# A recurrent gated attention with a feed-forward block on one core: a planned order of steps replaced by another

## The chip, the cores and the metric

The kernel runs on one core of one Trainium2 chip. The time is device microseconds of one execution of the whole program. The core has five engines with an instruction queue each: TensorE (PE), VectorE (DVE), ScalarE (ACT), GpSimd (POOL) and SyncE (SP), which only issues transfers here. Each engine runs its own queue in order, and waits for the others by semaphores.

## The reference

```python
def _attn_ref(q, k, v, alpha):              # (4, 8, 768, 48) each
    B, H, S, D = q.shape
    state = np.zeros((B, H, D, D), dtype=np.float32)
    y = np.zeros_like(q)
    for t in range(S):
        state = alpha[:, :, t, :, None] * state + np.einsum('bhd,bhe->bhde', k[:, :, t], v[:, :, t])
        y[:, :, t] = np.einsum('bhd,bhde->bhe', q[:, :, t], state)
    return y.astype(np.float32)

def _moe_ref(x, w_in, w_out):               # (3072, 384), (384, 2048), (2048, 384)
    h = x @ w_in
    g = h * np.cos(h)
    return (g @ w_out).astype(np.float32)
```

The output of the recurrence, with heads side by side, is the `x` of the second function. The result is 3072 x 384 in float32.

## The kernel before

*Tiling.* The sequence of 768 steps of each of 4 batches is cut into three pieces of 256, so there are 12 such pieces over all; the code calls the index `J`, and this text calls each a pair, because it holds two chunks (`c` = 0 and 1) of 128 steps. Within a chunk, steps lie two to a partition: the even or odd step is `e`. All 8 heads of 48 are handled together.

*The recurrence of a pair, step by step.* `load` brings alpha, k, q, v (393 KB each) through SP's queue. `mula` (line 149, POOL) multiplies neighbouring alphas, from pair 3 on. `ln` (L141, ACT) takes logarithms; `cums0` and `cums` (L155, L167, PE) sum them with triangular matrices; `sub` (L182, DVE) makes the sums of even steps from those of odd ones; `icp` and `exps` (L192, L200, ACT) take exponentials of both signs, and `eb` is these four and the next pair's `ln` as one step. `sk` and `sq` (L212, L216) scale k and q by them, on DVE where the plan has `:D`, else on POOL. `castv` (L219, POOL) makes v bfloat16; its two halves are stacked into `vs` by four transfers of SP (`vst`, L225) or, for pairs 0 to 2, by products with the identity (`vpe`, L235, and an eviction `vev`, L239). `decay` (L244, POOL) prepares the chunk's decay. `trans` (L260, PE) transposes k and q, `evT` (L266) evicts its two halves, `scores` (L274, PE) and `mask` (L279, DVE) make the masked scores of each chunk, `outer` (L291, PE) the outer products of k and v, `add` (L305, L307, DVE) and `state` (L313, POOL) the running state, `yT` (L340, PE) the output of the recurrence, transposed, and `evy` (L350) evicts its halves into `xT`.

*The feed-forward block of a pair.* `m1` (L359, PE) makes four units `h_ps` of 128 x 1024 (12 products each); `sin` (L365, ACT) their cosine; `gate` (L370, DVE) the product of the two; `m2` (L387, PE; L381 for the last chunk) multiplies by the second weight in four parts per chunk; `evo` (L396) evicts a chunk's result, and `out` (L403) stores it. The weights come through POOL's queue, in four quarters each (`w1`, `w2`; L121, L127), as needed first by pair 0.

*Buffers.* Most products write one of three PSUM buffers (tag `h`, two banks each: `h_ps`, `T_ps`, `A_ps`, `U_ps`, `y_ps`, `vs_ps`, and the first sums). A product that takes such a buffer waits until what was in it has been read: `m1` waits for a `gate` or a `mask` three uses earlier, for example. `m2` has one buffer (tag `o`), `cums` from pair 3 on one (tag `x`). The second half of a tile that is written by another engine waits for the first half (`evT 0` and `evT 1` write one tile, `evy 0` and `evy 1` too).

*Products of zeros.* `idle` (L411) multiplies zeros by zeros into a buffer that nothing reads, as often as the plan says, during the first 19 us.

*What sets the order.* A table, `PLAN` (L428 to L493), has a row for each kind of step (with the chunk, half or unit as second word) and a number for each of the 12 pairs; a letter behind a number names the engine (`A` ACT, `D` DVE; POOL or the step's own engine without one). The steps are issued in the order of these numbers over all rows, with the products of zeros (`IDLE`: number, how many) among them. So the numbers only sort: every engine's queue, SP's and POOL's too, is the part of this one list that it has to run. They are no times of the chip. The load of pair 2's alpha is also made to wait for the last product of `yT` of pair 1 (`GATES`, L99).

Of the kernel before, what the change touches and what calls it, by code (L numbers as in the profile page):

```python
# [16 lines left out]
def kernel(  # L17
# [11 lines left out]
    B, H, S, D = q.shape  # L29
# [64 lines left out]
    w1 = consts.tile([C, KT, DF], BF, tag="w1", name="w1")  # L94
    w2 = consts.tile([C, NF, DM], BF, tag="w2", name="w2")
# [311 lines left out]
    def idle(n):  # L407
# [21 lines left out]
        "load a": "1320 1974 27415 27985 34270 40270 43270 54870 67336 68770 70970 93397",  # L429
        "load k": "750 2544 28555 37270 46270 52480 58570 69470 72470 85140 91627 113474",  # L430
        "load q": "5250 6750 29125 38770 48970 56370 57870 60070 78470 84570 87104 96187",
        "load v": "3750 8250 35770 41770 51910 61570 67906 73970 75470 85710 95267 96757",
        "w1": "15334 12769 17804 16954",
        "w2": "11919 20284 19434 21134",
        "mula": "- - - 36680 41180 47582 54280 61956 76220 87867 79850 105765",
        "ln": "6160 7660 35857 38802 - - - - - - - -",
        "cums0": "7065 8565 36762 - - - - - - - - -",
        "cums": "7385 8885 37082 40224 45645 52564 65189 75864 86319 101370 105687 126624",
        "sub": "- - - 41095 48653 53084 68143 79971 86910 101948 106207 127144",
        "icp 0": "8400 10365 37282 - - - - - - - - -",  # L440
        "icp 1": "9990 9615 38042 - - - - - - - - -",
        "exps 0": "11510 9085 37657 - - - - - - - - -",
        "exps 1": "10740 11125 38417 - - - - - - - - -",
        "eb": "- - - 43138 49360 59320 71283 83790 88947 103219 109067 127741",
        "sk 0": "8970:D 11125:D 38180 44230 53330 64626 74150 90547 93387 106715 109595 129364:D",
        "sk 1": "10655:D 10185:D 38612:D 45094:D 52380 60226 77170 88817 96837 110545 113395 132041",
        "sq 0": "12160:D 14753:D 40150:D 45680:D 56671:D 65155:D 78900 85074 95107 111495 112445 133161",
        "sq 1": "12974:D 14283:D 39680:D 45680 55230 63676 75100 86024 91497 114515 116415 129403",
        "castv": "10660 16184 42680 48680 62906 71716 73380 94337 92617 104995 130491 144063",
# [90 lines left out]
```

## Time and profile before

| | |
|---|---|
| three runs | 189.58, 189.61, 190.51 us (median 189.61) |
| the profiled execution, its own time | 189.73 us |
| its span, first to last instruction | 187.7 us |
| granted TensorE clock, mean | 0.997 |
| TensorE busy from 0 to 22.2, 22.2 to 122, 122 to 187.7 us | 18.78, 96.96, 61.45 us |
| DVE, ACT, POOL busy over the span | 134.3, 125.3, 77.4 us |
| share of the 16 DMA engines, 0 to 100 us | 1.0 or more in each stage (0.69 from 100 to 122, 0.20 behind) |
| transfers | 29.47 MB in 60537 packets, 51424 of them under 512 B |

The profile is one execution. Its page has the busy time of each engine, the work in 40 slices, the transfer queues, the chain of work that ended last, and the costliest groups of instructions; the trace behind it gives each instruction's start and length and who ended a wait. A line of a timeline reads: start in us, length in us, engine, source line, operation, output and inputs, how many were merged, and in brackets the idle time before it and what ended that. Lengths of products are modelled at their end, so that neighbouring ones overlap. A row of waits reads: who waited for whom, us in total, how often, the longest.

### The profile page before, as it was taken

The page shows a single profiled execution, that of the slowest core. Times are in us where ns is not written, and L with a number is a line of the kernel's source. Part 1 is how long each engine was busy: PE and PEld are TensorE (multiplying, and loading weights), DVE is VectorE, ACT ScalarE, POOL GpSimd, SP SyncE. Part 2 cuts the span into 40 slices and gives each one's busy share as a digit, 9 for nine tenths or more (in the row PEclk, how much of TensorE's full clock was granted, in tenths as well). Part 3 has the DMA queues.
Part 4 walks back from the last instruction along what each step waited for, and adds up shares of the span by engine and source line. Part 5 has one row for each costly group of instructions (what it writes and reads, how often), then busy time and mean ns, then how long its engine had stood idle before and what let it go on. Part 6 is the DMA issues. An engine that isn't in the chain of part 4 may idle for free.

```text
span 187.7 us, 5795 instructions
## 1 busy us (share of the span) xinstructions
PE 177.2 (94%) x2471; PEld 126.7 (67%) x2474; DVE 134.3 (72%) x184; ACT 125.3 (67%) x161; POOL 77.4 (41%) x110
## 2 busy tenths in 40 slices
PE   7997799998999999999999999999999999999990
PEld 2444678664577776775688668686776786776880
DVE  7069775589799899589657986885876666573550
ACT  2466876899598977788577999728956182372520
POOL 5059610257664733783894068830540310100000
PEclk9999999999999999999999999999999999999998
DMA  6999999999959988996799943600042005501303
GB/s 152 261 256 154 185 203 236 255 264 265 249 137 302 265 184 217 265 268 166 195 280 259 216 106 90 166 0 3 3 114 73 0 21 124 128 1 45 84 0 84
DMA packets 60537, 29.47 MB, mean 157 GB/s; under 512 B 51424, under 2 KB 60512, under 8 KB 60512
## 3 DMA queue, kind: packets, MB, share of 16 engines
q1 hardware_dynamic: 56640, 25.86, 59.8%
q0 software_dynamic: 3712, 3.15, 11.0%
q8 instruction: 19, 0.31, 0.7%
q10 hardware_dynamic: 160, 0.10, 0.2%
q14 instruction: 6, 0.05, 0.1%
HBM read 25.17 MB, written 4.72 MB: 159 GB/s over the span
## 4 chain that ended last, share of the span: by engine, by line
PE 71%; ACT 16%; DVE 7%; issue 3%; DVEq 0%
PE h_ps L359 31%; PE o_ps L387 23%; PE idle_ps L411 5%; PE y_ps L340 3%; ACT c_sb L365 3%; ACT qkT L266 3%; DVE gsb L370 3%; PE T_ps L260 2%; ACT cp L200 2%; ACT L136 2%; ACT L365 2%; PE A_ps L274 2%; PE U_ps L291 2%; ACT lna L141 2%; ACT icp L192 2%
## 5 line engine op out<-in xcount | busy, mean ns | idle before, releaser
L370 DVE TENSOR_TENSOR gsb<-h_ps,c_sb 128x1024 bf16<-128x1024 f32 x48 | 58.1, 1221 | 22.3 <-ACT c_sb L365 21.5
L365 ACT ACTIVATE c_sb<-h_ps,halfpi 128x1024 bf16<-128x1024 f32 x48 | 53.0, 1113 | 27.4 <-PE h_ps L359 23.4
L359 PE MATMUL h_ps<-xT,w 128*128 128x256 bf16 x576 | 66.7, 273 | 1.4 <-issue 0.6
L387 PE MATMUL o_ps<-w,gsb 128*128 128x384 bf16 x368 | 66.7, 326 | 0.0
L359 PEld LDWEIGHTS <-w 128*128 128x128 bf16 x576 | 55.6, 98 | 10.4 <-issue 1.9
L387 PEld LDWEIGHTS <-gsb 128*128 128x128 bf16 x368 | 33.8, 98 | 21.2 <-DVE gsb L370 0.6
L313 POOL TENSOR_TENSOR un<-us,c 128x384 bf16<-128x384 f32 x20 | 16.8, 843 | 40.3 <-DVE us L305 33.9
L279 DVE TENSOR_TENSOR A_sb<-A_ps,msk 128x1024 bf16<-128x1024 f32 x24 | 28.9, 1216 | 1.3 <-PE A_ps L274 1.3
L212 POOL TENSOR_TENSOR kh<-k,icp 128x384 bf16<-128x384 f32 x17 | 16.9, 999 | 8.7 <-ACT icp L192 8.7
L216 POOL TENSOR_TENSOR qh<-q,cp 128x384 bf16<-128x384 f32 x15 | 15.4, 1032 | 10.9 <-ACT cp L200 10.9
L149 POOL TENSOR_TENSOR a<-a 128x384 f32<-128x384 f32 x9 | 9.3, 1037 | 12.9 <-DMA a<-in_alpha_dram 12.9
L411 PE MATMUL idle_ps<-zeros 128*128 128x512 bf16 x42 | 12.7, 445 | 1.6 <-DVE zeros L52 1.2
L219 POOL CAST vp<-v 128x768 bf16<-128x768 f32 x12 | 9.9, 824 | 9.0 <-DMA v<-in_v_dram 8.9
L141 ACT ACTIVATE lna<-a 128x768 bf16<-128x768 f32 x12 | 10.2, 846 | 4.5 <-DMA a<-in_alpha_dram 4.5
L136 ACT ACT_TABLE_LOAD x9 | 11.5, 1283 | 0.9 <-PEq L524 0.7
L266 ACT COPY qkT<-T_ps 128x1024 bf16<-128x1024 bf16 x8 | 8.0, 1016 | 6.2 <-PE T_ps L260 3.8
L266 DVE COPY qkT<-T_ps 128x1024 bf16<-128x1024 bf16 x16 | 10.8, 682 | 1.3 <-ACT qkT L266 1.3
L365 ACT ACT_TABLE_LOAD x9 | 11.5, 1283 | 0.2
L305 DVE TENSOR_TENSOR us<-U_ps,un 128x384 f32<-128x384 f32 x16 | 8.7, 550 | 3.8 <-PE U_ps L291 2.8
L396 DVE COPY o_sb<-o_ps 128x384 f32<-128x384 f32 x12 | 6.6, 552 | 6.6 <-PE o_ps L387 6.6
L274 PE MATMUL A_ps<-qkT 48*128 48x128 bf16 x192 | 9.2, 218 | 1.0 <-ACT vs L239 0.6
L396 ACT COPY o_sb<-o_ps 128x384 f32<-128x384 f32 x11 | 5.3, 478 | 7.1 <-PE o_ps L387 5.2
(69 smaller groups left out, 155.1 us busy)
## 6 DMA issues: line engine op xcount, KB each, us to landing
k<-in_k_dram SPq DMA_DIRECT2D x12, 384.0 KB, 5.5
a<-in_alpha_dram SPq DMA_DIRECT2D x12, 384.0 KB, 5.9
v<-in_v_dram SPq DMA_DIRECT2D x12, 384.0 KB, 6.2
q<-in_q_dram SPq DMA_DIRECT2D x12, 384.0 KB, 6.0
out_dram<-o_sb SPq DMA_DIRECT2D x46, 96.0 KB, 2.7
vs<-vp SPq DMA_DIRECT2D x36, 64.0 KB, 2.0
w<-in_moe_w_out_dram POOLq DMA_DIRECT2D x4, 384.0 KB, 9.9
w<-in_moe_w_in_dram POOLq DMA_DIRECT2D x4, 384.0 KB, 7.0
```

Source lines behind the costliest of these rows:

```text
L136: nc.scalar.preload_act_table_set("natural_log_exp_and_others")
L141: nc.scalar.activation(out=lna_t[J % NL][:, :, :, 0:D].rearrange("p e h d -> p h e d"), in_=a_sb.pop(J), func=AF.Ln)
L212: eng.tensor_tensor(out=kh_t[J % NQ][:, e, :, 0:D], in0=kqv["k", J][:, :, e], in1=icp_, op=ALU.mult)
L216: eng.tensor_tensor(out=qh_t[J % NQ][:, e, :, 0:D], in0=kqv["q", J][:, :, e], in1=cp, op=ALU.mult)
L266: copy(out=qkT_sb[J][:, c], in_=T_ps[J][:, c].rearrange("r n e s -> r n (e s)"))
L279: nc.vector.tensor_tensor(out=A_sb[J][:, c].rearrange("s a p t -> s (a p) t"), in0=A_ps.pop((J, c)).rearrange("s a p t -> s (a p) t"), in1 ...
L313: nc.gpsimd.tensor_tensor(out=u, in0=U_sum.pop(n), in1=c2_sb[J][:, :, c].unsqueeze(3).to_broadcast([C, NP, 2, D]), op=ALU.mult)
L359: nc.tensor.matmul(h_ps[J, u][:, f, :], w1[:, kk, ft * C : (ft + 1) * C], xT[J][:, kk, :], start=(kk == 0), stop=(kk == KT - 1))
L365: nc.scalar.activation(out=c_sb[J, u], in_=h_ps[J, u], func=AF.Sin, bias=halfpi, scale=1.0)
L370: nc.vector.tensor_tensor(out=gsb[J][:, u * FW : (u + 1) * FW], in0=h_ps.pop((J, u)), in1=c_sb.pop((J, u)), op=ALU.mult)
L387: nc.tensor.matmul(o_ps[J, c][:, 0:DM], gsb[J][:, ft, c * C : (c + 1) * C], w2[:, ft], start=(ft == 0), stop=(ft == NF - 1))
L411: nc.tensor.matmul(idle_ps[0], zeros[:, 0:C], zeros, start=True, stop=True)
```

## The change

The numbers of the plan are replaced: all rows of `PLAN`, some of the letters that name an engine, and `IDLE`. No function changes. The new numbers were chosen by the mean over drawn delays of transfers and engines. In the order that comes of them: alpha of pairs 0 and 1 is loaded ahead of k of pair 0; the first wait has 10 products of zeros and not 21, and the later ones are divided differently (36 in all, not 45); the first weights are issued earlier on POOL, the order of the eight quarters is another, and the last one stands behind `state 0` of pair 1; some steps are on other engines (the second eviction of `T_ps` of pair 0 on DVE, both evictions into `xT` of pairs 0, 1 and 11 on ACT, both scalings of k of pair 3 on POOL, the second eviction of pair 5 into `xT` and the second of pair 9 out of `T_ps` on ACT, and more); `mula` of pairs 9 to 11 and the load of pair 11's alpha are earlier, and the stores of the first outputs later. Shown are the rows that the steps below speak of.

```diff
-        "load a": "1320 1974 27415 27985 34270 40270 43270 54870 67336 68770 70970 93397",
-        "load k": "750 2544 28555 37270 46270 52480 58570 69470 72470 85140 91627 113474",
-        "load q": "5250 6750 29125 38770 48970 56370 57870 60070 78470 84570 87104 96187",
-        "load v": "3750 8250 35770 41770 51910 61570 67906 73970 75470 85710 95267 96757",
-        "w1": "15334 12769 17804 16954",
-        "w2": "11919 20284 19434 21134",
-        "mula": "- - - 36680 41180 47582 54280 61956 76220 87867 79850 105765",
-        "ln": "6160 7660 35857 38802 - - - - - - - -",
-        "cums0": "7065 8565 36762 - - - - - - - - -",
-        "cums": "7385 8885 37082 40224 45645 52564 65189 75864 86319 101370 105687 126624",
...
-        "icp 0": "8400 10365 37282 - - - - - - - - -",
...
-        "exps 0": "11510 9085 37657 - - - - - - - - -",
...
-        "sk 0": "8970:D 11125:D 38180 44230 53330 64626 74150 90547 93387 106715 109595 129364:D",
-        "sk 1": "10655:D 10185:D 38612:D 45094:D 52380 60226 77170 88817 96837 110545 113395 132041",
-        "sq 0": "12160:D 14753:D 40150:D 45680:D 56671:D 65155:D 78900 85074 95107 111495 112445 133161",
-        "sq 1": "12974:D 14283:D 39680:D 45680 55230 63676 75100 86024 91497 114515 116415 129403",
-        "castv": "10660 16184 42680 48680 62906 71716 73380 94337 92617 104995 130491 144063",
...
-        "vpe": "12269 19888 44159 - - - - - - - - -",
-        "vev": "15703:A 20408:A 45777:A - - - - - - - - -",
...
-        "trans": "14073 17773 40885 47348 58944 70064 80866 92234 109989 116249 127239 136001",
-        "evT 0": "14773:A 18473:A 41585 48048 60976 71899 81566:A 93894 111044 116949:A 129834 138061",
-        "evT 1": "16453:A 19403:A 43330 48048:A 59896 72979 81586 93289 112124 117657 128759 137201:A",
-        "scores 0": "16168 19573 43514 48885 69514 73578 83495 102418 118225 127719 141861 153101",
...
-        "outer": "11844 21513 43734 50168 69734 87367 83935 102638 115919 118665 142081 152771",
-        "add 0": "13808 22948 46150 50743 70284 87917 86435 103563 117182 119805 142631 155397",
-        "add 1": "15551 24515 - 53559 72504 - 88392 107822 - 121420 145386 -",
-        "state 0": "14460 23600 46802 51395 70936 89767 87087 104215 121237 120457 143283 156049",
...
-        "yT": "20503 26545 48000 58219 72693 91349 90719 109104 124433 140168 151138 162701",
-        "evy 0": "21333:D 27535:D 49128:D 60501:D 73683 92814:D 91919 110094:D 125423 140998 152879:D 163777:D",
-        "evy 1": "21333 27658 48990 59421:D 73683:D 92339:D 91549 110569:D 125793 141368 152128 163814",
...
-        "m1 2": "27430 29401 54182 61235 78800 96763 104369 120396 132629 149072 159970 166198",
...
-        "gate 2": "30097 32068 57141 64015 82191 99430 108297 125521 135296 151739 162637 168865",
...
-        "evo 1": "40620:D 52358:D 69619 83600:D 99289 111649:D 124538 136831 148962 159862 170328:D 179531:D",
-        "out 0": "47770 53670 76970 97327 92197 114044 134921 150722 154222 155552 167028 178835",
-        "out 1": "44770 66136 87674 100827 112274 133721 136121 156752 149522 168228 170958 180161",
-    IDLE = [(1501, 21), (7915, 1), (9416, 8), (12569, 4), (14554, 5), (16389, 3), (18254, 3)]
+        "load a": "750 1320 27361 27931 34507 40507 48007 52492 57802 68607 72007 77577",
+        "load k": "1890 2460 28501 37507 43507 60407 67907 69307 77007 86952 100211 116963",
+        "load q": "5250 6750 29071 39007 45007 53062 61907 62607 81407 99071 99641 126980",
+        "load v": "3750 8250 36007 42007 46507 57232 59572 78147 85812 86382 96101 107230",
+        "w1": "13312 11442 17539 12292",
+        "w2": "19239 20089 18389 24326",
+        "mula": "- - - 36917 41417 48312 56502 58222 76409 75459 78358 83017",
+        "ln": "4660 6160 35481 38949 - - - - - - - -",
+        "cums0": "5565 7065 36909 - - - - - - - - -",
+        "cums": "7915 7385 37229 40371 45970 54264 62935 80853 87354 101752 106479 114900",
...
+        "icp 0": "9105 7585 37814 - - - - - - - - -",
...
+        "exps 0": "9480 7960 37429 - - - - - - - - -",
...
+        "sk 0": "10228:D 9160 38417:D 44417 53652 66517 73739 85353 94526:D 112075 119991 128667",
+        "sk 1": "9300:D 14516:D 38887:D 45367 52532 67467 77408 87243 94996:D 105350 110355 131715:D",
+        "sq 0": "12705:D 15055 39917:D 45917:D 55552 61849:D 79308 89951 91071 113025 123059 131840",
+        "sq 1": "12160:D 13897:D 40387:D 46317 54602 68417 75680:D 87212:D 92021 109436:D 114145 130890",
+        "castv": "10660 16769 43147 49262 57452 74689 65017 86473 106300 111305 103630 118344",
...
+        "vpe": "11707 17804 45260 - - - - - - - - -",
+        "vev": "15222:A 18324:A 45907:A - - - - - - - - -",
...
+        "trans": "13592 18199 41122 47671 58673 70446 81901 92616 110371 117254 126968 136383",
+        "evT 0": "14292:A 19074:A 41822 48371 61244 71943:A 82601:A 93316 112031 117954 130073 138443",
+        "evT 1": "15766 20004:A 43567 48371:A 59689 72873:A 83342 93921 111426 117954:A 128328 137083:A",
+        "scores 0": "16142 20174 43751 49267 69896 73960 84097 102800 118907 127448 142573 153483",
...
+        "outer": "12102 21894 44087 50550 70116 87969 84317 103020 117734 119347 142243 153153",
+        "add 0": "13422 22894 45331 51100 70692 88519 85597 103887 118559 121627 143603 153736",
+        "add 1": "15291 24461 - 52715 72307 - 90134 105977 - 123194 145218 -",
+        "state 0": "14162 23546 47362 51752 71344 89171 88339 104570 119211 122279 144255 154388",
...
+        "yT": "20489 26491 48382 57948 73075 91731 91101 109486 125115 139897 150867 159129",
+        "evy 0": "21319 27604 49372:D 60294:D 74065 92721:D 92301 110951:D 126475 140985:D 154211:D 160489",
+        "evy 1": "21689 27974 49372 60769:D 74065:D 92721 91931 110476:D 126105 140727 153261:D 160119",
...
+        "m1 2": "27589 29025 54564 61617 79535 97145 104751 121078 132358 149454 161332 165274",
...
+        "gate 2": "30256 31692 57231 64397 82202 99872 108296 123745 135025 152121 163999 170935",
...
+        "evo 1": "40857:D 55472 70217:D 83982:D 98353 114003 125220 136488 145700 159234:D 173346 179908:D",
+        "out 0": "58372 70507 73507 97871 96671 115763 119572 149760 161064 162264 169976 179142",
+        "out 1": "64107 56032 94901 84612 107800 114563 125780 137048 146260 159864 173906 180538",
+    IDLE = [(1501, 10), (5885, 2), (8445, 10), (12433, 2), (14072, 6), (16726, 2), (18679, 4)]
```

## The prediction

> **What bounds the kernel now.** I read the page first (parts 1, 4 and 5), then the timeline of the first 24 us, then the waits of TensorE after that, then the places where TensorE waited.
>
> ```profile
> PE 177.2 (94%) x2471; PEld 126.7 (67%) x2474; DVE 134.3 (72%) x184; ACT 125.3 (67%) x161; POOL 77.4 (41%) x110
> L411 PE MATMUL idle_ps<-zeros 128*128 128x512 bf16 x42 | 12.7, 445 | 1.6 <-DVE zeros L52 1.2
> ```
>
> TensorE is the bound, but 12.7 us of its 177.2 are products of zeros (L411), all in the first 19 us. So there are two regimes: up to 22.25 us, where the first `h_ps` product starts (pair 0, unit 1), a latency chain over all engines sets the time; from there to the last product, which ends at 183.45, TensorE runs nearly packed. The first regime, from the timeline:
>
> ```profile
> 1.20 7.00 PE L411 MATMUL idle_ps<-zeros 128*128 128x512 bf16 x21 [1.20 <-DVE zeros L52]
> 5.86 0.84 ACT L141 ACTIVATE lna<-a 128x768 bf16<-128x768 f32 x1 [3.83 <-DMA a<-in_alpha_dram]
> 7.36 0.84 ACT L141 ACTIVATE lna<-a 128x768 bf16<-128x768 f32 x1 [0.67 <-DMA a<-in_alpha_dram]
> ...
> 9.06 0.49 ACT L192 ACTIVATE icp<-cums_h 128x384 f32<-128x384 f32 x1 [0.85 <-PE cums_h L167]
> ...
> 12.96 1.03 DVE L216 TENSOR_TENSOR qh<-q,cp 128x384 bf16<-128x384 f32 x2 [0.37 <-ACT cp L200]
> ...
> 14.54 1.01 ACT L266 COPY qkT<-T_ps 128x1024 bf16<-128x1024 bf16 x1 [1.61 <-PE T_ps L260]
> ...
> 16.74 2.36 DVE L279 TENSOR_TENSOR A_sb<-A_ps,msk 128x1024 bf16<-128x1024 f32 x2 [0.24 <-PE A_ps L274]
> ...
> 20.27 0.35 PE L340 MATMUL y_ps<-qkT,un 128*32 128x128 bf16 x12 [0.23 <-ACT qkT L266]
> ...
> 21.72 0.48 ACT L350 CAST xT<-y_ps 128x384 bf16<-128x384 f32 x1 [0.79 <-DVE xT L350]
> ```
>
> The reader is to see that the first logarithm was done at 6.70, while TensorE was still in its 21 zeros until 8.20; and that the second half of `xT` (pair 0) waited for the first although another engine wrote it.
>
> In the second regime the waits of TensorE that the profile names after 22 us are few:
>
> ```profile
> PE h_ps L359 <- issue: 0.6, 1, 0.6
> PE U_ps L291 <- DVE gsb L370: 0.6, 2, 0.4
> PE h_ps L359 <- ACT xT L350: 0.5, 1, 0.5
> PE U_ps L291 <- DVE xT L350: 0.4, 1, 0.4
> PE cums L155 <- ACT lna L141: 0.4, 1, 0.4
> PE T_ps L260 <- DVE gsb L370: 0.3, 1, 0.3
> ```
>
> The 0.5 for `xT` is the start at 22.25. The other five, 2.3 us, lie at 44.03, 46.51, 51.76, 86.52, 98.92 and 120.14. After 122 us there is none. So the change can gain in the first regime and in those 2.3 us, and nowhere else; what it can lose has no such limit.
>
> **The change, part by part.** No product of the calculation is added or removed; after 22 us only order and engines change.
>
> (1) *Loads.* The two alpha loads go ahead of the first k. Loads land one each 1.50 us (5.86 to 7.36 in the rows above), so they take the first and second place: 4.36 and 5.86. Both logarithms end 1.50 earlier, the second at 6.70. k of pair 0 lands at 7.36 in place of 4.4, still ahead of its use.
>
> (2) *Zeros.* Ten of them, at 7.00/21 = 0.33 on average and 0.43 while the clock is half (their weight loads come 0.43 apart until 5.86, then 0.2): 1.20 + 4.3 = 5.5. They no longer hold up the first sums; two more bridge to 6.7. The sums of pair 1 then need what they needed before, 9.10 to 10.13, or 1.03: the first exponential starts at 7.8 in place of 9.06. The eight exponentials took 3.87 with a wait of 0.58 in them, so 3.3: done at 11.1, not 12.93. The q scaling then waits for q itself, sixth to land, at 5.86 + 4 x 1.50 = 11.9, and not for `cp` (12.96): 1.0 earlier. [...]
>
> (3) *Steps of pairs 0 and 1.* The transposition follows the q scaling, so T_ps is evicted from 13.5, not 14.54. The second half of that eviction moves from ACT (1.03) to DVE (0.68), where it stands behind `add 1` of pair 0, which waits for POOL's `state 0`. POOL now issues three weight loads (0.75 to 0.80 each) after its cast of v (end 11.24) and before that: 11.24 + 2.4 + 0.42 (decay) + 0.84 = 15.0; add 0.55, copy 0.68: the first mask starts at 16.15, not 16.74. Here 0.4 of the 1.0 is given back. The scores of pair 1 then go through vpe, two evictions of T_ps on ACT (1.01 each), and `yT` of pair 0 starts behind the first, at 19.4 to 19.6, in place of 20.27, where it waited for the second. Both writes of `xT` are on ACT now, 0.86 for both as for pair 6 (94.17 to 95.03), where DVE after ACT took 1.07: another 0.2. Sum: the first `h_ps` product at 21.2 to 21.4, a gain of 0.9 to 1.05.
>
> Against it: the weight loads are issued from 11.3 on, while q and v of pair 1 are still arriving. In the view of the DMA engines from 10 to 20 us they ran at 260 GB/s until 14.0, fell to between 15 and 126 for some 1.5 us, and then carried the weights at 200. The earlier issue fills that hole, so the weights end 1.5 earlier, but v of pair 1 (cast at 16.37) shares with the first of them. If it lands 2 us later than now (some 14.8, as eighth by the spacing), the cast (0.84), vpe (0.36), its eviction (0.82) and the first T_ps eviction (1.01) follow one after another to 19.9, and the gain is 0.4. [...] I take 0.9 as the gain, ends 0.4 and 1.1.
>
> (4) *22 to 58 us.* The order here is nearly the old one. What sets it is ACT's chain, with a table load of 1.28 on each change between Sin and Exp, and `trans` of pair 3. The wait at 44.03 (0.23) goes, as `outer` of pair 2 is asked for later. A k scaling of pair 3 moves from DVE (0.60) to POOL (1.00), ahead of the q scaling (1.27) that `trans` needs and of pair 2's `state 0`; that costs up to 1.0 and returns 0.6 on DVE, where the q scaling took 1.35 beside POOL's. The 0.45 at 51.76 goes, as ACT writes `xT` last there and DVE no longer. I take a gain of 0.2; ends +0.9 (all waits) and -1.0 (POOL's 1.00).
>
> (5) *58 to 122 us.* The wait at 86.52 (0.35) goes: DVE's copy waited 0.90 for ACT's half of the same tile, with a gate behind it; that gate now goes first. At 120.14 (0.30) one gate fewer lies in front of `trans` of pair 9, but its second copy goes to ACT behind DVE's half: from DVE's 0.68 and ACT's 1.02 the next `outer` comes 0.45 late. For pair 5 the second `xT` write goes to ACT behind DVE's (0.56 + 0.48), then a table load (1.28), Sin (1.11) and gate (1.22), before unit 2's products may write: 4.8 against 4.4 of products, a loss of 0.4. Sum: 0.35 + 0.30 - 0.45 - 0.4 = -0.2. The 0.62 "issue" at 98.92 has no releaser; it may recur anywhere. I count half, +0.3, ends 0 and 0.6.
>
> (6) *122 us to the end.* No wait before; order moved by a few steps; 0, ends 0 and -0.6.
>
> Sum: 0.9 + 0.2 - 0.2 + 0.3 = 1.2 us. The profiled execution took 189.73 with a span of 187.70 (2.03 around it); 189.73 - 1.2 = 188.5, and the median shown (189.61) stands 0.1 under it, so I say **188.5 us**. With all good ends: 1.1 + 0.9 + 0.65 + 0.6 = 3.25, or 186.4; with all bad ones: 0.4 - 1.0 - 0.85 - 0.6 = -2.05, or 191.7.
>
> **The rivals.**
> *No change (189.5).* The gain at the front is eaten at 36 to 40 us. There `ln` of pair 2 and `mula` of pair 3 need alpha, which lands only behind the last weight (`mula` waited 12.0 us in this trace, until 36.17). The last w2 quarter is now behind `state 0` of pair 1 on POOL. For: SP's k load took 4.39 to issue there. Against: the other seven weights come earlier. Time: 189.7 - 0.2 = 189.5.
>
> *Slower (191.1).* A load blocks POOL's queue: `mula` of pair 11 now stands ahead of the k scaling of pair 7 and `state 0` of pair 6, and its alpha comes right behind k of pair 8. In the old run that place in SP's queue was at 77.3; one more stacking of v (2.8) and one more store (2.0) stand ahead of it now, so 82 at the old pace. Alpha took 5.9 at the median and 8.3 at the most from issue to landing: 87.9 to 90.3. Behind it POOL has 1.0 + 1.0 + 0.21 + 0.82 + 1.0 + 0.83 = 4.9 up to the end of that `state 0`: 92.8 to 95.2. `yT` of pair 6, which needs it, ran at 93.31 and would run at 92.1: a loss of 0.7 to 3.1. It decides from a landing at 87.2. Taken at 2.6: 188.5 + 2.6 = 191.1. For: POOL's queue has nothing else to do first. Against: with the weights 1.5 earlier the median landing is 86.4, which is in time.
>
> *Cold array (189.0).* If the clock stays half past 9 us, the two bridging zeros cost 0.21 more each and the four 384-column sums 0.16 more each: 1.1 later exponentials, of which q's arrival hides 0.8; the transposition and scores of pair 0 add some 0.2. So 188.5 + 0.5 = 189.0.
>
> **How the numbers follow.** What a measurement of this kernel can tell from no change is about 0.5%, or 0.95 us: faster is below 188.66. Forecast 0.50 (of it 0.44 faster, 0.06 same; its own range 187.2 to 189.1), no change 0.18 (0.14 same, 0.04 slower), blocked POOL 0.24 (0.06 same, 0.18 slower), cold array 0.08 (0.02 faster, 0.05 same, 0.01 slower). Faster 0.46, same 0.31, slower 0.23. The range 187.2 to 191.2 leaves out a tenth on each side.
>
> **What would show it.** Logarithms at 4.4 and 5.9; clock full near 5.9; the first exponential near 7.8; the first mask near 16.2; the first `h_ps` product between 21.2 and 21.9; the alpha of pair 2 landed by 33; `outer` of pairs 2 and 6 without a wait; a wait of 0.4 ahead of unit 2 of pair 5. The prediction fails if TensorE waits over 0.5 us at `trans` of pairs 5 or 6 or `yT` of pair 6 behind POOL, or if the first `h_ps` product is not before 22.

## The result and the profile after

The changed kernel took 191.59 us (median of 8, 190.34 to 192.26) against 189.81 (median of 8, 189.24 to 190.51) for the kernel before on the same chip: a ratio of 1.0087, 95% interval 1.0058 to 1.0115. The forecast was 188.5, with a range of 187.2 to 191.2: the change made the kernel slower, not faster. The profiled execution took 191.62 with a span of 189.6.

First the page of the changed kernel: two rows of busy time by engine and group, one row of a group that was too small to show before, and the granted clock in 40 slices of 4.74 us.

```profile
PE 176.7 (93%) x2463; PEld 126.6 (67%) x2465; DVE 136.7 (72%) x180; ACT 128.2 (68%) x167; POOL 76.7 (40%) x108
L411 PE MATMUL idle_ps<-zeros 128*128 128x512 bf16 x34 | 11.5, 483 | 1.5 <-DVE halfpi L77 1.2
L212 DVE TENSOR_TENSOR kh<-k,icp 128x384 bf16<-128x384 f32 x8 | 7.7, 992 | 6.1 <-ACT icp L192 6.1
PEclk9999699999999999999999999999999999999999
```

TensorE is busy for 0.5 less than before while the span is 1.9 longer, so time was lost in waits. A k scaling on DVE costs 992 ns in the mean; a lone one takes 0.55. The fifth slice of the clock is a 6. Both are looked up in the timeline of the first 25 us (start, length, engine, line, operation, tiles, idle time before and its releaser):

```profile
1.20 4.45 PE L411 MATMUL idle_ps<-zeros 128*128 128x512 bf16 x10 [1.20 <-DVE halfpi L77]
4.40 0.84 ACT L141 ACTIVATE lna<-a 128x768 bf16<-128x768 f32 x1 [2.38 <-DMA a<-in_alpha_dram]
5.91 0.84 ACT L141 ACTIVATE lna<-a 128x768 bf16<-128x768 f32 x1 [0.66 <-DMA a<-in_alpha_dram]
7.83 0.49 ACT L192 ACTIVATE icp<-cums_h 128x384 f32<-128x384 f32 x1 [1.08 <-PE cums_h L167]
12.02 1.03 DVE L216 TENSOR_TENSOR qh<-q,cp 128x384 bf16<-128x384 f32 x2 [1.07 <-DMA q<-in_q_dram]
...
13.45 0.56 DVE L216 TENSOR_TENSOR qh<-q,cp 128x384 bf16<-128x384 f32 x1
13.46 0.80 POOL L121 DMA_DIRECT2D w<-in_moe_w_in_dram  x1
13.93 3.33 DVE L212 TENSOR_TENSOR kh<-k,icp 128x384 bf16<-128x384 f32 x1
14.28 0.84 POOL L313 TENSOR_TENSOR un<-us,c 128x384 bf16<-128x384 f32 x1
15.07 1.00 POOL L216 TENSOR_TENSOR qh<-q,cp 128x384 bf16<-128x384 f32 x1
16.01 0.82 POOL L219 CAST vp<-v 128x768 bf16<-128x768 f32 x1
16.78 0.80 POOL L121 DMA_DIRECT2D w<-in_moe_w_in_dram  x1
17.18 0.55 DVE L305 TENSOR_TENSOR us<-U_ps,un 128x384 f32<-128x384 f32 x1
17.65 0.68 DVE L266 COPY qkT<-T_ps 128x1024 bf16<-128x1024 bf16 x1
...
18.38 0.40 PE L274 MATMUL A_ps<-qkT 48*128 48x128 bf16 x8 [2.58 <-DVE qkT L266]
20.50 1.89 PE L411 MATMUL idle_ps<-zeros 128*128 128x512 bf16 x4
22.86 0.36 PE L340 MATMUL y_ps<-qkT,un 128*32 128x128 bf16 x12
24.70 1.05 PE L359 MATMUL h_ps<-xT,w 128*128 128x256 bf16 x8
```

The first five rows are as forecast. Then one step goes wrong: the second k scaling of pair 1 stands on DVE from 13.93 to 17.26, while POOL runs its state step, a q scaling and the cast of v one after the other. Behind it in DVE's queue wait `add 1` and the copy of the second half of `T_ps`, both of pair 0, and for that copy the scores of pair 0's second chunk on TensorE: 18.38, where they stood at 17.39 before. The first `h_ps` product starts at 24.70, not 22.25. In the kernel before, that k scaling was the first of the three at 11.03, and the step that ran on DVE beside the state step was the second q scaling of two (it started at 14.84 and took 1.19):

```profile
11.03 1.56 DVE L212 TENSOR_TENSOR kh<-k,icp 128x384 bf16<-128x384 f32 x3 [0.89 <-ACT icp L192]
...
14.37 1.66 DVE L216 TENSOR_TENSOR qh<-q,cp 128x384 bf16<-128x384 f32 x2
14.61 1.01 POOL L313 TENSOR_TENSOR un<-us,c 128x384 bf16<-128x384 f32 x1
...
17.39 0.40 PE L274 MATMUL A_ps<-qkT 48*128 48x128 bf16 x8
```

The clock, in a view of stretches cut where its grants changed (length, then busy time by engine, granted clock, DMA share, GB/s); first the changed kernel, then the one before:

```profile
core 0: us, PE busy (x) PEld busy (x) DVE busy (x) ACT busy (x) POOL busy (x), PEclk, DMA share, GB/s
12.69:16.11 3.42, 2.70 (x47) 1.34 (x46) 3.42 (x4) 1.71 (x2) 3.38 (x6) 1.00 1.23 198
16.11:19.52 3.41, 0.98 (x13) 0.45 (x14) 3.41 (x5) 0.00 (x0) 3.41 (x5) 1.00 1.18 180
19.52:22.94 3.42, 3.42 (x53) 1.74 (x52) 1.06 (x1) 2.73 (x3) 1.36 (x3) 0.50 1.22 192
```

```profile
12.70:16.11 3.41, 2.82 (x44) 1.34 (x44) 3.15 (x6) 1.80 (x3) 3.26 (x5) 1.00 1.00 153
16.11:19.52 3.41, 2.70 (x59) 1.55 (x61) 2.74 (x3) 2.28 (x4) 3.39 (x6) 1.00 1.25 199
```

In the 3.41 us up to 19.52 the stalled TensorE was busy for 0.98, and the next 3.41 ran at half clock. In them four zeros took 1.89, 0.47 each, and the scores of pair 1 stood behind them until 22.32, some 0.7 after ACT's copy for them had ended (it started at 20.61 and took 1.0).

After that the two kernels run nearly alike. The longer of TensorE's waits from 22 us to the end of the changed kernel (who for whom, us in total, times, longest):

```profile
PE h_ps L359 <- DVE gsb L370: 0.8, 2, 0.5
PE T_ps L260 <- DVE qh L216: 0.6, 1, 0.6
PE A_ps L274 <- DVE us L305: 0.4, 1, 0.4
```

The lateness of the changed kernel against the one before, wherever both had just finished the same set of TensorE steps (from the two traces):

| time in the kernel before, us | 23.7 | 42.2 | 57.4 | 62.0 | 87.0 | 100.3 | 101.6 | 110.6 | 132.8 | end |
|---|---|---|---|---|---|---|---|---|---|---|
| late by, us | 2.47 | 3.10 | 1.57 | 2.27 | 2.07 | 1.27 | 1.70 | 1.57 | 2.02 | 1.92 |

So 2.47 us are lost before 24 us, and 0.55 come back until the end.

### The profile page after: what moved, and what is told of

It is laid out like the page before. It is cut to its first block, busy times and chain, and to the rows that moved or that the text cites. A ratio compares the mean times of both kernels' runs of the same rounds, so it can differ in the third digit from the quotient of the medians.

```text
span 189.6 us, 5782 instructions
## 1 busy us (share of the span) xinstructions
PE 176.7 (93%) x2463; PEld 126.6 (67%) x2465; DVE 136.7 (72%) x180; ACT 128.2 (68%) x167; POOL 76.7 (40%) x108
## 4 chain that ended last, share of the span: by engine, by line
PE 50%; ACT 15%; DMA 10%; SPq 8%; DVE 8%; issue 5%; POOL 2%; DVEq 0%; POOLq 0%
PE o_ps L387 20%; PE h_ps L359 20%; SPq L105 5%; ACT c_sb L365 5%; DMA q<-in_q_dram 3%; DMA k<-in_k_dram 3%; DMA a<-in_alpha_dram 3%; PE y_ps L340 3%; DVE gsb L370 2%; SPq L403 2%; ACT L365 2%; ACT cp L200 2%; PE A_ps L274 2%; DVE qh L216 2%; ACT L136 2%
## 5 line engine op out<-in xcount | busy, mean ns | idle before, releaser
L370 DVE TENSOR_TENSOR gsb<-h_ps,c_sb 128x1024 bf16<-128x1024 f32 x48 | 58.1, 1222 | 22.7 <-ACT c_sb L365 21.7
L359 PE MATMUL h_ps<-xT,w 128*128 128x256 bf16 x576 | 67.4, 273 | 1.1 <-DVE gsb L370 0.8
L279 DVE TENSOR_TENSOR A_sb<-A_ps,msk 128x1024 bf16<-128x1024 f32 x24 | 28.9, 1216 | 4.7 <-PE A_ps L274 4.6
L212 POOL TENSOR_TENSOR kh<-k,icp 128x384 bf16<-128x384 f32 x16 | 16.2, 1017 | 17.6 <-ACT icp L192 10.9
L219 POOL CAST vp<-v 128x768 bf16<-128x768 f32 x12 | 10.2, 849 | 14.9 <-PE U_ps L291 9.5
L216 POOL TENSOR_TENSOR qh<-q,cp 128x384 bf16<-128x384 f32 x14 | 14.5, 1042 | 1.3 <-DMA q<-in_q_dram 1.3
L266 ACT COPY qkT<-T_ps 128x1024 bf16<-128x1024 bf16 x9 | 8.9, 1015 | 7.7 <-DVE qkT L266 4.2
L396 ACT COPY o_sb<-o_ps 128x384 f32<-128x384 f32 x14 | 6.7, 478 | 10.3 <-PE o_ps L387 10.2
L411 PE MATMUL idle_ps<-zeros 128*128 128x512 bf16 x34 | 11.5, 483 | 1.5 <-DVE halfpi L77 1.2
L212 DVE TENSOR_TENSOR kh<-k,icp 128x384 bf16<-128x384 f32 x8 | 7.7, 992 | 6.1 <-ACT icp L192 6.1
L274 PEld LDWEIGHTS <-qkT 48*128 48x128 bf16 x192 | 5.9, 95 | 8.5 <-issue 3.3
L266 DVE COPY qkT<-T_ps 128x1024 bf16<-128x1024 bf16 x15 | 10.1, 682 | 0.8 <-ACT qkT L266 0.5
```

What stands on the lines that cost most here:

```text
L212: eng.tensor_tensor(out=kh_t[J % NQ][:, e, :, 0:D], in0=kqv["k", J][:, :, e], in1=icp_, op=ALU.mult)
L216: eng.tensor_tensor(out=qh_t[J % NQ][:, e, :, 0:D], in0=kqv["q", J][:, :, e], in1=cp, op=ALU.mult)
L266: copy(out=qkT_sb[J][:, c], in_=T_ps[J][:, c].rearrange("r n e s -> r n (e s)"))
L274: nc.tensor.matmul(A_ps[J, c][:, a, p, :], qkT[r, c, NP + p, :], qkT[r, c, p, :], start=True, stop=True)
L279: nc.vector.tensor_tensor(out=A_sb[J][:, c].rearrange("s a p t -> s (a p) t"), in0=A_ps.pop((J, c)).rearrange("s a p t -> s (a p) t"), in1 ...
L359: nc.tensor.matmul(h_ps[J, u][:, f, :], w1[:, kk, ft * C : (ft + 1) * C], xT[J][:, kk, :], start=(kk == 0), stop=(kk == KT - 1))
```

## The experiments

Each edit replaces numbers of the plan; the products of the calculation stay the same in all of them. Times are medians; ratios are to the kernel before, measured again beside each (189.9 to 190.1 us), with 95% intervals. The lines shown of a timeline are picked and need not be neighbours.

| | kernel | us | ratio |
|---|---|---|---|
| 1 | k scaling early | 188.25 | 0.991 (0.989 to 0.994) |
| 2 | zeros during the stall | 191.23 | 1.006 (1.003 to 1.008) |
| 3 | new order up to 27 us, then the old | 192.24 | 1.013 (1.009 to 1.017) |
| 4 | old order up to 27 us, then the new | 189.30 | 0.996 (0.994 to 0.998) |
| 5 | a load issued between state and q scaling | 190.36 | 1.000 (0.997 to 1.003) |
| 6 | the load ahead of the state step moved behind | 189.35 | 0.995 (0.993 to 0.997) |
| 7 | the old kernel with 10 first zeros | 189.39 | 0.995 (0.994 to 0.997) |
| 8 | 1, and two evictions back | 187.95 | 0.988 (0.987 to 0.990) |
| 9 | the two scalings exchanged | 192.33 | 1.012 (1.009 to 1.015) |
| 10 | zeros during the stall, 36 in all | 191.83 | 1.009 (1.007 to 1.012) |
| 11 | k scaling on POOL | 191.06 | 1.006 (1.004 to 1.008) |
| 12 | 8, and one weight load later | 189.37 | 0.996 (0.993 to 0.999) |

**1. The k scaling of pair 1 early on DVE.**

```diff
-        "sk 1": "9300:D 14516:D 38887:D 45367 52532 67467 77408 87243 94996:D 105350 110355 131715:D",
+        "sk 1": "9300:D 11000:D 38887:D 45367 52532 67467 77408 87243 94996:D 105350 110355 131715:D",
```

> The changed kernel with one step moved: the second k scaling of pair 1 (L212 on DVE) goes back to an early place in DVE's order, ahead of both q scalings, where it stood before the change; nothing else differs. Theory S (stall): that scaling took 3.33 us instead of 0.55 because GpSimd worked beside it, this kept TensorE idle for 2.6 us, and the idle time cost the clock for 3.4 us more. S expects the scaling to be over by about 12.1 us, the scores of pair 0's second chunk near 16.4 instead of 18.4, no half clock after 6 us, the first h_ps product at 21.2 to 21.5 instead of 24.70, and so 191.6 - 3.3 = 188.3 us (187.9 to 188.8). Theory Z (zeros): the clock falls because fewer zeros run at the start, whatever DVE does; then the half clock of 19.5 to 22.9 stays and the time is 190.3 to 191.6. Theory O (order of the work after 27 us costs the time): no change, 191.3 to 191.9.

188.25 us. From the timeline:

```profile
14.39 0.84 POOL L313 TENSOR_TENSOR un<-us,c 128x384 bf16<-128x384 f32 x1
15.27 0.56 DVE L305 TENSOR_TENSOR us<-U_ps,un 128x384 f32<-128x384 f32 x1 [1.14 <-POOL un L313]
16.48 0.40 PE L274 MATMUL A_ps<-qkT 48*128 48x128 bf16 x8 [0.57 <-DVE qkT L266]
21.68 4.00 PE L359 MATMUL h_ps<-xT,w 128*128 128x256 bf16 x34
```

DVE now idles until the state step ends, as the prediction had it, the scores follow at 16.48, and the clock stays full from 6.03 to the end of the work. In its new place the scaling started at 10.98, beside the cast of v, and took 1.17; the q scaling behind it started 0.09 after its q had landed (0.10 in the changed kernel), so this cost nothing that the trace shows. The first `h_ps` product came at 21.68, 0.2 behind the expected 21.2 to 21.5. Theory S holds; Z and O fall as causes of the loss. One number of a plan of several hundred made the difference between slower and faster.

**2 and 10. Only the clock.** Zeros fill the stall; the stall stays.

```diff
-    IDLE = [(1501, 10), (5885, 2), (8445, 10), (12433, 2), (14072, 6), (16726, 2), (18679, 4)]
+    IDLE = [(1501, 10), (5885, 2), (8445, 10), (12433, 2), (14072, 6), (16300, 11), (16726, 2), (18679, 4)]
```

> The changed kernel with 11 more products of zeros on TensorE between the two score steps of pair 0, where it was idle from 15.8 to 18.4 us (11 x 0.213 = 2.3 us); the stalled scaling on DVE is left as it is. Theory S splits the loss into two parts: the stall, which stays, and the half clock, which these zeros prevent. It expects the scaling at 3.3 us again, a full clock from 6 us on, and 191.6 - 1.3 = 190.3 us (190.0 to 190.7), as the one execution of the changed kernel with a granted clock of 0.999 took 190.34. If the half clock cost nothing of its own (the evictions on ScalarE and VectorE set the time there), 191.6 stays. Theory Z expects the half clock again somewhere in 10 to 25 us.

```profile
13.97 3.33 DVE L212 TENSOR_TENSOR kh<-k,icp 128x384 bf16<-128x384 f32 x1
15.78 2.55 PE L411 MATMUL idle_ps<-zeros 128*128 128x512 bf16 x10
18.42 0.40 PE L274 MATMUL A_ps<-qkT 48*128 48x128 bf16 x8
23.63 2.14 PE L359 MATMUL h_ps<-xT,w 128*128 128x256 bf16 x18
```

The clock stayed full and the first `h_ps` product came 1.07 earlier than in the changed kernel, but the time, 191.23, fell by only 0.36 (by the two ratios 0.6, and their intervals overlap). The trace shows where the rest went: a wait of 0.92 without a releaser at 98.96 to 99.88, which the changed kernel doesn't have in that size. The tenth kernel was to keep that place as it was:

```diff
-    IDLE = [(1501, 10), (5885, 2), (8445, 10), (12433, 2), (14072, 6), (16726, 2), (18679, 4)]
+    IDLE = [(1501, 10), (5885, 2), (8445, 10), (14072, 6), (16300, 10)]
```

> The second experiment again (zeros while DVE is stalled), but with as many zeros in all as the changed kernel has, 36: ten stand between the two score steps of pair 0, and ten smaller fillers are taken away (2 ahead of the first transposition, 2 and 4 behind the second score step). In the second experiment the first h_ps product came 1.07 earlier (23.63 against 24.70), yet the time fell by only 0.36, as a wait of 0.92 without a releaser stood at the 1364th matmul of TensorE's stream; the changed kernel, with eleven fewer zeros, had a wait of 0.27 there. Theory S: the half clock costs 1.1 us; with the count as in the changed kernel the gap is 0.3 again, and the time is 191.6 - 1.1 = 190.5 us (190.1 to 190.9). If the gap does not go by the count of instructions: 191.0 to 191.5.

```profile
17.74:21.16 3.42, 1.69 (x46) 0.95 (x44) 2.98 (x4) 1.64 (x2) 3.27 (x5) 1.00 1.19 190
21.16:24.57 3.41, 3.18 (x77) 2.61 (x78) 1.92 (x2) 2.29 (x5) 0.00 (x0) 0.50 1.27 203
```

191.83: the wait near the 1365th product was 0.27, as in the changed kernel, but the zeros that were taken away left TensorE busy for only 1.69 of the 3.42 us up to 21.16, and the next 3.41 ran at half clock. So it didn't single out the clock. What is left for its price is the 1.07 of the second kernel's trace, the one execution of the changed kernel with a mean clock of 0.999 in place of 0.990 to 0.991 (190.34 against 191.36 to 192.26), and the executions of the fifth kernel (below).

**3 and 4. Which part of the order.** The plans are cut at 26.8 on their scale, where both have run the same steps; one half is taken from each. One row of the third kernel (the fourth has it the other way round):

```diff
-        "trans": "13592 18199 41122 47671 58673 70446 81901 92616 110371 117254 126968 136383",
+        "trans": "13592 18199 40885 47348 58944 70064 80866 92234 109989 116249 127239 136001",
```

> The order of the changed kernel for all steps of the first 27 us on every engine, and the order of the kernel before for everything after. Theory S: the whole loss lies in the first 27 us, and the new order after that is worth a gain of about 0.5 us, which is missing here: 191.6 + 0.5 = 192.1 us (191.7 to 192.6), with the first h_ps product at 24.7. Theory O (the order after 27 us costs the time): 189.0 to 190.5.

> The reverse: the order of the kernel before for the first 27 us, and the order of the changed kernel for everything after. Theory S: 189.8 - 0.5 = 189.3 us (188.9 to 189.8), with the first h_ps product at 22.25 as before. Theory O: 191.0 or more.

192.24 and 189.30, both as theory S has it: the new order after 27 us is worth 0.4% (0.2 to 0.6), the first 27 us cost all the rest. The third kernel's scaling took 3.33 too.

**5 and 6. POOL's order beside the scaling.** DVE's order is that of the changed kernel.

```diff
-        "w1": "13312 11442 17539 12292",
+        "w1": "13312 11442 14600 12292",
```

> The changed kernel with one weight load (the third quarter of w1) issued by GpSimd between its state step and its q scaling, and no longer after the cast of v; DVE's order is left alone. In the changed kernel the slow k scaling on DVE ended 0.43 after the last of three GpSimd steps in a row (state, q scaling, cast), while GpSimd was issuing a load. Theory S (DVE waits for as long as GpSimd computes without a break, and an issue is a break): the scaling ends 0.4 after the state step, near 15.55, so it takes 1.6 us and not 3.33; the scores of pair 0's second chunk come near 16.7, the clock stays full, the cast of v and all behind it come 0.4 later than in the kernel with the early scaling: first h_ps product near 22.1 and 188.7 us (188.3 to 189.3). Rival W (the scaling is slow for a cause of its own, such as the weights' traffic or a place in DVE's order): it takes 3.3 us again, and the time is 191 or more. Rival Q (DVE waits until GpSimd's queue holds no more computing): it ends 0.4 after the later cast, near 18.1, and the time is 192 or more.

```profile
13.93 2.23 DVE L212 TENSOR_TENSOR kh<-k,icp 128x384 bf16<-128x384 f32 x1
14.28 0.85 POOL L313 TENSOR_TENSOR un<-us,c 128x384 bf16<-128x384 f32 x1
15.06 0.80 POOL L121 DMA_DIRECT2D w<-in_moe_w_in_dram  x1
15.88 1.13 POOL L216 TENSOR_TENSOR qh<-q,cp 128x384 bf16<-128x384 f32 x1
```

The scaling ended at 16.16, 1.1 earlier than in the changed kernel: not 3.3 (W), not 18.1 (Q), but also not 15.55, as S had it. The state step had ended at 15.13; DVE's scaling was over only 0.30 after the issue behind it (15.06 to 15.86). TensorE then idled 1.49, the clock fell after a stretch of 3.41 us with 1.51 busy, and the time was 190.36. The twelve executions of this kernel also price the clock: seven with a mean clock of 0.986 to 0.991 took 190.30 to 191.19 (median 190.64), five with 0.998 or more 188.87 to 189.86 (median 189.25), so 1.4 us apart in one and the same kernel. Where in time the clock fell, and what else differed, is known for the profiled one alone.

```diff
-        "w1": "13312 11442 17539 12292",
+        "w1": "16800 11442 17539 12292",
```

> The changed kernel with one weight load (the first quarter of w1) issued behind GpSimd's cast of v of pair 1, and no longer ahead of the state step. GpSimd's state step is then ready at 13.55, while DVE's q scaling of pair 1 runs (13.45 to 14.01). In most other places of the traces a scaling on DVE waited for one GpSimd step and ended 0.41 after it, and the next GpSimd step was the one to wait (1.31 in place of 1.00); only here it lost three times in a row. Theory T (they take turns, and the load issued just ahead broke the turn): the k scaling ends 0.4 after the state step, near 15.2, and takes 1.2 us; the q scaling of GpSimd takes 1.3; first h_ps near 21.6 and 188.3 us (187.9 to 188.9). Theory R (a run of ready GpSimd steps always goes first): the scaling ends 0.4 after the cast of v, near 16.9, taking 2.9 us; first h_ps near 23.5 to 24.3 and 190 to 191.5 us.

```profile
13.50 0.56 DVE L216 TENSOR_TENSOR qh<-q,cp 128x384 bf16<-128x384 f32 x1
13.70 1.05 POOL L313 TENSOR_TENSOR un<-us,c 128x384 bf16<-128x384 f32 x1
13.97 1.19 DVE L212 TENSOR_TENSOR kh<-k,icp 128x384 bf16<-128x384 f32 x1
14.71 1.31 POOL L216 TENSOR_TENSOR qh<-q,cp 128x384 bf16<-128x384 f32 x1
```

Theory T to the tenth, and not R: the scaling takes 1.19 and ends 0.41 after the state step, then POOL's q scaling waits and takes 1.31. No DVE step was moved. The first `h_ps` product started at 21.49. The time, 189.35, is 1.0 over the forecast: the later load landed at 23.40 and `h_ps` waited 0.5 for it, and the wait near the 1365th product was 0.50.

**7. Fewer zeros alone.**

```diff
-    IDLE = [(1501, 21), (7915, 1), (9416, 8), (12569, 4), (14554, 5), (16389, 3), (18254, 3)]
+    IDLE = [(1501, 10), (7915, 1), (9416, 8), (12569, 4), (14554, 5), (16389, 3), (18254, 3)]
```

> The kernel before with the first wait filled by 10 products of zeros in place of 21, and nothing else of the change. Theory S: the loss has nothing to do with these zeros. The first sums start at 6.75 in place of 8.03, the exponentials of pair 0 come up to 1.2 earlier, those of pair 1 still wait for the second logarithm at 8.20; the q scaling comes 0 to 0.9 earlier, so 189.0 to 190.0 us, with a full clock after 6 us. Theory Z (fewer zeros bring the clock down later): a half clock of 3.4 us in the records within the first 25 us and 190.5 us or more.

189.39, in the range of S, but not by its mechanism. In the trace the clock was half from 7.54 to 10.95, as theory Z had it, after 3.41 us in which TensorE was busy for 42%; but the first `h_ps` product came at 22.40, only 0.15 late. The time came back at 99 us, where the wait of 0.62 of the kernel before is 0.09. So this trace tells of that wait, and not of the front. (Three of the twelve executions had a mean clock of 0.986 to 0.991, the profiled one among them: 189.35 to 189.78, against 188.67 to 189.81 for the others.)

**8. The two evictions.** Against the first kernel:

```diff
-        "evT 1": "15766 20004:A 43567 48371:A 59689 72873:A 83342 93921 111426 117954:A 128328 137083:A",
+        "evT 1": "15766 20004:A 43567 48371:A 59689 72873:A 83342 93921 111426 117954 128328 137083:A",
-        "evy 1": "21689 27974 49372 60769:D 74065:D 92721 91931 110476:D 126105 140727 153261:D 160119",
+        "evy 1": "21689 27974 49372 60769:D 74065:D 92721:D 91931 110476:D 126105 140727 153261:D 160119",
```

> The changed kernel with the k scaling of pair 1 early on DVE (as in the first experiment, 188.25 us) and two evictions back on the engines that they had before: the second xT write of pair 5 on DVE, and the second T_ps eviction of pair 9 on DVE. In the changed kernel TensorE waits 0.44 at 101.3 for a gate ahead of unit 2 of pair 5, and 0.6 and 0.4 at 123.7 and 124.5 in pairs 8 and 9. The prediction put these at 0.4 and 0.45 (each net of what the change saved there). Expected if it was right: both waits go, 188.25 - 0.85 = 187.4 us (187.1 to 187.9). If the waits only move on to the next step, as DVE is the later engine there: 188.0 to 188.6.

187.95, the fastest of all, 0.3 under the first kernel and not 0.85 (the intervals of the two ratios overlap). The wait in pair 5 went (0.42 between the two traces). In pair 9 it changed its name: the scores now wait 0.50 for that very copy on DVE, and the lateness there is the same.

**9. The step or the place?**

```diff
-        "sk 1": "9300:D 14516:D 38887:D 45367 52532 67467 77408 87243 94996:D 105350 110355 131715:D",
+        "sk 1": "9300:D 13600:D 38887:D 45367 52532 67467 77408 87243 94996:D 105350 110355 131715:D",
```

> The changed kernel with two neighbours on DVE exchanged: the k scaling of pair 1 now stands ahead of the q scaling of pair 1 (both of them multiply two tiles in SBUF, both are needed by the transposition of pair 1 alone). If the 3.33 us belong to the place and not to the step (GpSimd's run of state, q scaling and cast starts while the second of the two waits), the k scaling takes 0.56 and the q scaling behind it takes 3.2 to 3.4, and the time stays at 191.0 to 191.9 us. If they belong to the k scaling (its data, its tile), it is slow in its new place too, and ends near 16.8.

```profile
13.45 0.55 DVE L212 TENSOR_TENSOR kh<-k,icp 128x384 bf16<-128x384 f32 x1
13.92 3.36 DVE L216 TENSOR_TENSOR qh<-q,cp 128x384 bf16<-128x384 f32 x1
```

The place. The k scaling is as short as any, and the q scaling behind it is stalled. (The time, 192.33, has 0.6 more for a wait of `trans` of pair 6 for POOL's q scaling at 86.3 us; this wait was 0.3 or less in the changed kernel, and 0.4 to 0.8 in the first, ninth and tenth.)

**11 and 12. Other ways round the stall.** First the scaling on POOL, with two weight loads behind the cast of v:

```diff
-        "w1": "13312 11442 17539 12292",
+        "w1": "16950 11442 17539 16900",
-        "sk 1": "9300:D 14516:D 38887:D 45367 52532 67467 77408 87243 94996:D 105350 110355 131715:D",
+        "sk 1": "9300:D 10700:P 38887:D 45367 52532 67467 77408 87243 94996:D 105350 110355 131715:D",
```

> The changed kernel with the k scaling of pair 1 on GpSimd, behind its cast of v of pair 0 (near 11.6 to 12.6), and with two of the three weight loads that GpSimd issued ahead of its state step moved behind its cast of v of pair 1. So DVE has one scaling of two SBUF tiles less, and the state step starts near 13.9 in place of 14.28. Theory S: first h_ps product 0.2 to 0.5 earlier than in the kernel with the early scaling on DVE (21.68): 21.2 to 21.5, and 187.8 to 188.2 us. The price could be the weights: they come 1.3 to 4 us later, and if the second or third quarter of w1 is late for its unit (first products at 22 to 25 us) the gain is lost: 188.3 to 189.5.

Then the eighth kernel with the last quarter of w1 later and the first earlier:

```diff
-        "w1": "13312 11442 17539 12292",
+        "w1": "12292 11442 17539 16800",
```

> The kernel of the eighth experiment (187.95 us) with one weight load, the last quarter of w1, issued by GpSimd behind its cast of v of pair 1 and no longer ahead of its state step, and the first quarter issued second. In the sixth experiment the same was done with the first quarter: no issue stood in front of the state step, which then came 0.6 earlier, and DVE and GpSimd took turns; but that quarter landed at 23.40, 0.5 after TensorE asked for it. The last quarter is asked for 1.4 later, near 24.0. Expected from that: the state step at 13.7, the scores of pair 0's second chunk near 15.95 in place of 16.58, the first h_ps product near 21.2 in place of 21.79, no wait for weights, and 187.95 - 0.5 = 187.4 us (187.1 to 187.8). If the later load pushes the second quarter and the w2 loads back so that a product waits, the gain is lost: 187.9 to 188.5.

191.06 and 189.37: both missed, above even the ranges for late weights. In the eleventh TensorE waited

```profile
PE h_ps L359 <- DMA w<-in_moe_w_in_dram: 1.2, 1, 1.2
```

and by 51 us it had lost 1.2 more against the first kernel, 0.6 of it in one wait for the logarithm of alpha of pair 2, which landed 3.6 later (37.53 in place of 33.97). In the twelfth the front was 0.59 faster, as expected (first `h_ps` product 21.20), and no product waited for w1. But the w2 quarter that is issued third landed at 33.10 in place of 30.19, `m2` waited 0.7 for it, alpha of pair 2 came 1.9 later behind it, and by 57 us the kernel was 1.5 behind the eighth. The load issued 2.8 us later left a hole that nothing filled: from 18 to 24 us the transfers ran at 139 GB/s in place of 189, and over the first 36 us at 202 in place of 212. In this order, then, early weight loads are worth more than an earlier front; what they are worth in the old order was not tried.

## Why the prediction was wrong

*What bounds the kernel, loads, zeros:* right. Logarithms at 4.40 and 5.91, zeros over at 5.65 (5.5), first exponential 7.83 (7.8), q landed at 11.92 (11.9) and its scaling started at 12.02, clock full at 5.87 as before.

*Part (3) failed, in the sentence "15.0; add 0.55, copy 0.68: the first mask starts at 16.15".* The end of the state step was right (15.12; the terms as listed add up to 14.9). But the sentence put nothing between it and `add 1`. The change moved the second k scaling of pair 1 from 11.03 on DVE to the place right ahead of `add 1`; the prediction doesn't name that move. At its usual 0.55 it would have been over at 14.5, hidden behind the state step. Beside POOL it took 3.33, and the mask started at 18.25 (16.34 in experiment 1, without the stall). The prediction's own sign of failure, a first `h_ps` product not before 22, came: 24.70. The trace of before had the warning: the q scaling at 14.84 took 1.19 beside the state step, another at 46.14 took 1.35 beside POOL's q scaling, and part (4) even used that 1.35. At the front it was not asked which POOL steps would now lie beside which DVE steps.

The traces also show which DVE steps were touched: in the changed kernel the scalings (L212 and L216, both inputs in SBUF) took 0.55 to 3.33, and the 48 gates (L370), 24 masks (L279) and 16 additions (L305), which read one input from PSUM, stayed within 1.21 to 1.23, 1.21 to 1.23 and 0.54 to 0.56 whatever POOL did. The trace of before has the same split: 0.55 to 1.35 for the scalings, and 1.21 to 1.23, 1.21 to 1.23 and 0.54 to 0.56 for the same numbers of gates, masks and additions. By that the place on DVE was to be doubted; what causes the split was not shown.

*The size of it:* without the stall the first `h_ps` product starts at 21.68 (experiment 1): a gain of 0.57, where 0.9 was forecast with ends of 0.4 and 1.1. With it 1.95 are lost (21.68 to 23.63, experiments 1 and 2), and the half clock adds 1.07 (to 24.70; 1.4 by the executions of experiment 5). So the term +0.9 came out at -2.45, and the sum of 1.2 at -1.9.

*v of pair 1:* landed at 14.83, the 14.8 that its place in the row gave, so the first weight load (issued 11.57, landed 17.06) did not delay it; the rival value of 0.4 for that part was not needed.

*Part (4), 22 to 58 us:* a gain of 0.2 was forecast; the lateness went from 2.47 to 2.27 at 62 us. That the sizes agree is in part luck: the wait at 51.76 is gone, as forecast, but a new one of 0.55 at 59.48, for a gate, which the prediction did not name, came in its place (in the table 1.57 to 2.27), and one of 0.55 at 44.01, for a q scaling on DVE, was given back by 46 us.

*Part (5):* the wait at 86.52 is gone, and the 0.62 at 98.92 is not there (half was counted); unit 2 of pair 5 costs 0.43 of lateness (0.4 forecast, though the terms of its 4.8 add up to 4.65 and so to 0.25); pair 9 costs 0.45 (0.45 forecast, with 0.30 against it). From 62 to 133 us 0.25 was gained, where 0.1 was forecast. *Part (6):* 0.1, where 0 was forecast. So the second regime gained 0.55 where 0.3 was forecast; 0.78 of lateness went with the wait at 98.92 alone (2.05 to 1.27). Experiment 4, whose trace still has that wait (0.65), is yet faster by 0.4%.

*The rivals:* none named the stall. POOL's queue did stand still for the load of pair 11: it idled 2.89 ahead of that `mula`, until 0.13 after the landing at 89.06; but `yT` of pair 6 did not wait (95.36, with the lateness unchanged). Alpha of pair 2 landed at 34.76, not by 33 as the prediction asked (34.63 before); the lateness did not rise for it (2.47 at 24 us, 2.34 at 37 us of the kernel before). The half clock of the rival "cold array" came, but at 19.52 and by another way. A list of rivals that asks who waits for whom, step by step, leaves out a step that only gets slower by its neighbour on another engine.

## What to carry to other kernels

When a step moves, look not only at its queue but at what the other engines do beside it: here a scaling on DVE, with two inputs in SBUF, took 0.55 at its shortest and up to 3.36 beside a run of GpSimd steps, and a group whose mean is well over its minimum (992 ns against 546 for L212 in the changed kernel) shows this. The stall of TensorE near the start cost twice, 1.95 as time and 1.07 as clock; eleven products of zeros in it kept the clock (experiment 2, 191.23), and taking the stall away was better (experiment 1, 188.25). A planner that draws the delay of each step without regard to what the other engines do would not see such a coupling; that this is how the place was chosen was not tried. One misplaced step hid a gain of one per cent here.

## What the runs showed of the hardware

*Turns between DVE and GpSimd.* In the 14 profiles 93 scalings on DVE took 0.62 us or more, and 92 of them ended 0.41 or 0.42 after a GpSimd step; the next GpSimd step, where one followed at once, mostly took 0.31 longer (1.31 in place of 1.00). In the changed kernel and in experiments 2, 3, 9 and 10 it lost three times in a row (3.33 to 3.36 each). In all of these a weight load was issued just ahead of the state step; with that load elsewhere they took turns (experiment 6: 1.19 on DVE, then 1.31 on GpSimd). An earlier start did not help: in the changed kernel DVE's scaling started at 13.93 (the one ahead of it ended at 14.01), before the state step at 14.28, and still lost. In experiment 6 the state step also started 0.58 earlier, while DVE's q scaling ran, so whether the load or that start decides the turn is open, and so is the 2.23 of experiment 5.

*The clock went by stretches of 3.41 us, and a stretch need not be idle.* In the changed kernel the full clock was granted at 5.87, held for 13.65, which is four times 3.41, and was half from 19.52 to 22.94; stretches of 3.41 at half clock stand in experiments 5 (18.21 to 21.62), 7 (7.54 to 10.95) and 10 (21.16 to 24.57) too. Over the 14 profiles, counted in steps of 3.41 us from the first grant, on to 35 us and back to the first products, each stretch in which TensorE was busy for 24 to 49% of the time at full clock was followed by one at half clock, and none with 61% or more was. At half clock, 85% or more brought the full clock back, and 77% or less did not. The longest gap does not sort them: the stretch with 49% had none over 1.10 us, and one of 1.21 in a stretch with 64% left the clock full. So each fall came after a stretch in which TensorE had worked for part of the time.

*A wait that moves with the count of products.* TensorE waited 0.62 without a releaser after its 1365th recorded product in the kernel before, and in experiments 2, 3, 4 and 6 after the 1364th to 1367th for 0.50 to 0.92, while in the others it was 0.3 or less. Each of the five ended 1.3 to 1.6 us after a packet of 16,384 bytes of the instruction queue had landed. That the packet is the cause was not tried.
